# A retention block and two gated MLPs on one core: first loads held to three under way, first weights loaded and converted early, transposes of 64 rows in pairs, both banks of a phase as one tile

## The chip, the core and the metric

One core of a Trainium2 chip runs the whole program. Time is device microseconds (us) of one execution. The kernel before took a median of 939.42 us in 3 runs (938.97 to 939.46). The engines are PE (TensorE, with its weight loads as PEld), DVE (VectorE), ACT (ScalarE), POOL (GpSimd) and SP (SyncE, which here only issues DMAs). [...]

## The reference

Float32 throughout. Retention over 4 sequences of 576 positions with 8 heads of 64, then two MLPs over all 2304 tokens:

```python
gamma = 1.0 - 2.0 ** (-5.0 - np.arange(H))
Dmat = np.where(rel >= 0, gamma[:, None, None] ** rel, 0.0)      # rel = i - j
attn = ((q @ k.T) / sqrt(64) * Dmat) @ v                         # per sequence and head
x = attn as [2304, 512]
h = x @ w_in;  x = (h * sigmoid(1.702 * h)) @ w_out              # 512 -> 2048 -> 512
xn = x / sqrt(mean(x * x) + 1e-6) * rms_g
out = (silu(xn @ w_gate) * (xn @ w_val)) @ w_out2                # 512 -> 1536 -> 512
```

## The kernel before

**Tiling.** The tokens are cut into 18 units of 128 (two chunks of 64; `units`, L216). The MLPs work on blocks of 512 or 384 tokens (`BLOCKS`, L19). Matrix products of the MLPs are three passes over float32 values split into a high and a low part (`three`, L206). Weights arrive as 512 KB loads in six staging slots (`w_load`, L138), and `conv` (L168) turns each into such parts: two ACT instructions in place (L171, L172), one DVE instruction (`ww`, L181), then the high part (L188) and the low part (L191). With `rest` given, L188 runs on ACT and L191 is kept for a later call.

**A unit of attention** has three phases. `a_trans` (L259) transposes k and q on PE against an identity, ACT copies kT out of PSUM (L271), DVE multiplies qT by decay (L272) and POOL multiplies v by decay in place (L273). `a_scores` (L285) makes the 64x64 score blocks (L292) and the products of k and v (L301); DVE masks the scores into r (L307). `a_state` (L314) carries the running state S on DVE. `a_out` (L343) multiplies r by v (L352) and S by qT (L364); ACT copies x out of PSUM (L373), DVE adds the other half (L377), ACT and POOL or DVE split x into xh (L381) and xl (L383).

**Order.** Each engine runs its instructions in the order in which the code records them (`manual_schedule`). The front (L678 to L707) handles units 0 to 3 alone, phase after phase; then block 0 of the first MLP runs with its weight conversions and the phases of units 4 to 7 between its steps (L732), and blocks 1 to 3 run with the phases of units 8 to 17.

**Loads.** SP issues all loads in program order. The loads of units 0 to 3 stand there one after the other; those behind them go through `held` (L670): after each load, `behind` (L664) has SP issue a DMA of one word out of the load three before (`scrap`, L667), so that SP waits until that load has landed. Such a DMA reads the tile, so an instruction that later writes the tile in place (L273 for v, L171 and L172 for a staging slot) also waits until it is done.

**PSUM in the front.** A phase takes two tiles of one bank each (`a_psum`, L255): transposes from the pool `ps_at`, scores and outputs from `ps_acc`.

## Time and profile before

| | |
|---|---|
| median of 3 runs | 939.42 us (938.97 to 939.46) |
| profiled execution, and its span | 937.07 us, 935.3 us |
| PE busy | 922.1 us (99%) |
| DVE, ACT, POOL busy | 536.3, 377.6, 44.2 us (57%, 40%, 5%) |
| chain that ended last | PE 90%, DVE 5%, ACT 3%, issue 2% |
| transposes on that chain (L264) | 1% |

The span falls into three stretches: the front up to the first MLP matmul at 28.74 us, block 0 with the weight conversions up to about 130 us, and the rest. A time in the timeline is the start from the span's beginning and then the duration; what stands in brackets is the engine's idle time before it and what ended it ("issue" is a wait for nothing that the profile shows). Matmul durations overlap, so the pace of PE is read from start to start.

### The profile page before, as it was taken

What the parts mean: (1) busy time and instruction counts of PE and PEld (TensorE: products, weight loads), DVE (VectorE), ACT (ScalarE), POOL (GpSimd) and SP (SyncE); (2) the same over time, 40 slices, a digit from 0 to 9 for tenths busy, and PEclk for the clock granted to TensorE, in tenths of its full rate; (3) what the DMA queues carried; (4) which work ended last, traced back from release to release, by engine and by line L of the source; (5) the groups of instructions that cost most, each with busy time, mean ns of one, the idle gap of its engine ahead of it and who ended that gap; (6) DMA issues with size and microseconds to landing.
All of it is one profiled execution on the core that took longest, in us unless ns stands there. A gap on an engine that the chain in (4) does not pass through costs nothing.

```text
span 935.3 us, 15298 instructions
## 1 busy us (share of the span) xinstructions
PE 922.1 (99%) x6356; PEld 799.4 (85%) x6356; DVE 536.3 (57%) x885; ACT 377.6 (40%) x682; POOL 44.2 (5%) x47
## 2 busy tenths in 40 slices
PE   8899999999999999999999999999999999999998
PEld 7677788888999999988888888888888889999997
DVE  4888774444568555567777647464444544644333
ACT  3666654333444444466565523322332223223222
POOL 3111110000010010000000000000000000000000
PEclk9899999999999999999999999999999999999999
DMA  9866612101411324054455300200020001000000
GB/s 218 262 192 188 169 35 69 35 12 23 125 35 35 93 56 147 2 169 121 136 172 192 100 1 1 80 1 0 1 79 1 1 0 46 1 1 1 35 1 34
DMA packets 91579, 67.06 MB, mean 72 GB/s; under 512 B 58868, under 2 KB 81652, under 8 KB 91510
## 3 DMA queue, kind: packets, MB, share of 16 engines
q1 hardware_dynamic: 91074, 65.94, 23.8%
q8 instruction: 50, 0.82, 0.4%
q10 hardware_dynamic: 436, 0.14, 0.1%
q14 instruction: 19, 0.16, 0.1%
HBM read 55.59 MB, written 10.49 MB: 71 GB/s over the span
## 4 chain that ended last, share of the span: by engine, by line
PE 90%; DVE 5%; ACT 3%; issue 2%; DMA 0%; ACTq 0%; DVEq 0%
PE h L209 12%; PE acc L210 11%; PE acc L211 11%; PE acc L209 11%; PE h L211 11%; PE h L210 11%; PE v L209 5%; PE v L210 5%; PE v L211 5%; PE at L264 1%; DVE ww L181 1%; PE at L364 1%; PE at L292 1%; PE at L352 1%; DVE w L181 1%
## 5 line engine op out<-in xcount | busy, mean ns | idle before, releaser
L209 PE MATMUL h<-xh,w 128*128 128x512 f32 (+1 forms) x560 | 212.4, 379 | 2.1 <-ACT xh L381 2.1
L210 PE MATMUL h<-xl,w 128*128 128x512 f32 (+1 forms) x560 | 206.9, 369 | 0.3 <-DVE xl L383 0.3
L211 PE MATMUL h<-xh,w 128*128 128x512 f32 (+1 forms) x560 | 206.8, 369 | 0.0
L395 ACT CAST gh<-g 128x512 fp32r<-128x512 f32 (+1 forms) x140 | 80.9, 578 | 235.8 <-DVE g L546 152.9
L397 DVE TENSOR_TENSOR gl<-g,gh 128x512 fp32r<-128x512 f32 (+1 forms) x140 | 92.0, 658 | 79.5 <-ACT gh L395 79.5
L209 PEld LDWEIGHTS h<-xh,w 128*128 128x128 f32 x560 | 105.6, 188 | 18.6 <-ACT xh L381 2.4
L210 PEld LDWEIGHTS h<-xl,w 128*128 128x128 f32 x560 | 105.6, 189 | 14.9 <-issue 1.3
L203 DVE TENSOR_TENSOR wrl<-w,wrh 128x512 fp32r<-128x512 f32 x130 | 92.1, 709 | 45.5 <-ACT wrh L202 44.6
L211 PE MATMUL acc<-gh,wrl 128*128 128x512 f32 (+1 forms) x320 | 117.6, 367 | 0.0
L210 PE MATMUL acc<-gl,wrh 128*128 128x512 f32 (+1 forms) x320 | 117.5, 367 | 0.0
L209 PE MATMUL acc<-gh,wrh 128*128 128x512 f32 (+1 forms) x320 | 117.5, 367 | 0.0
L211 PEld LDWEIGHTS h<-xh,w 128*128 128x128 f32 x560 | 105.5, 188 | 13.5
L202 ACT CAST wrh<-w 128x512 fp32r<-128x512 f32 x130 | 80.4, 618 | 60.5 <-PE acc L211 45.1
L419 DVE TENSOR_TENSOR g<-h,g 128x512 f32<-128x512 f32 (+1 forms) x80 | 50.9, 636 | 72.8 <-ACT g L418 72.7
L209 PE MATMUL v<-xh,w 128*128 128x512 f32 (+1 forms) x240 | 88.1, 367 | 0.0
L210 PE MATMUL v<-xl,w 128*128 128x512 f32 (+1 forms) x240 | 88.1, 367 | 0.0
L211 PE MATMUL v<-xh,w 128*128 128x512 f32 (+1 forms) x240 | 88.1, 367 | 0.0
L418 ACT ACTIVATE g<-h 128x512 f32<-128x512 f32 (+1 forms) x80 | 44.2, 553 | 102.1 <-PE h L211 102.0
L211 PE MATMUL acc<-wrh,gl 128*128 128x512 f32 x216 | 84.5, 391 | 0.0
L210 PE MATMUL acc<-wrl,gh 128*128 128x512 f32 x216 | 84.5, 391 | 0.0
L209 PE MATMUL acc<-wrh,gh 128*128 128x512 f32 x216 | 84.0, 389 | 0.0
L543 DVE TENSOR_TENSOR g<-h,g 128x512 f32<-128x512 f32 (+1 forms) x60 | 38.2, 637 | 68.7 <-ACT g L542 68.6
(88 smaller groups left out, 1126.6 us busy)
## 6 DMA issues: line engine op xcount, KB each, us to landing
sslots<-in_moe_w_out_dram SPq DMA_DIRECT2D x28, 512.0 KB, 3.9
sslots<-in_moe_w_in_dram SPq DMA_DIRECT2D x16, 512.0 KB, 3.9
sslots<-in_moe_w_gate_dram SPq DMA_DIRECT2D x12, 512.0 KB, 3.9
sslots<-in_moe_w_val_dram SPq DMA_DIRECT2D x12, 512.0 KB, 4.3
out_dram<-sslots SPq DMA_DIRECT2D x17, 256.0 KB, 2.2
k<-in_k_dram SPq DMA_DIRECT2D x16, 256.0 KB, 3.4
q<-in_q_dram SPq DMA_DIRECT2D x16, 256.0 KB
v<-in_v_dram SPq DMA_DIRECT2D x16, 256.0 KB, 5.6
```

The lines of the kernel that those rows point to most:

```text
L181: nc.vector.scalar_tensor_tensor(out=w.bitcast(U32), in0=hi.bitcast(U32), scalar=3, in1=lo, op0=ALU.logical_shift_left, op1=ALU.bitwise_or,)
L202: nc.scalar.copy(out=wh.bitcast(F32R), in_=w)
L203: nc.vector.tensor_tensor(out=wl.bitcast(F32R), in0=w, in1=wh, op=ALU.subtract)
L209: nc.tensor.matmul(ps, lh, rh, start=first, stop=False)
L210: nc.tensor.matmul(ps, lh, rl, start=False, stop=False)
L211: nc.tensor.matmul(ps, ll, rh, start=False, stop=last)
L264: nc.tensor.transpose(pt[i][:, p * 128:(p + 1) * 128], t[:, 2 * p:2 * p + 2, :].rearrange("p h d -> p (h d)"), ident,)
L395: nc.scalar.copy(out=gh, in_=g)
L397: nc.vector.tensor_tensor(out=gl, in0=g, in1=gh.bitcast(F32), op=ALU.subtract)
L418: nc.scalar.activation(out=g, in_=ps, func=AF.Sigmoid, scale=1.702)
L419: nc.vector.tensor_tensor(out=g, in0=ps, in1=g, op=ALU.mult)
L543: nc.vector.tensor_tensor(out=g, in0=pg, in1=g, op=ALU.mult)
```

## The change

The loads of all four first units go through `held`, and the first 512 KB of `w_in` go right behind unit 0's k, q and v. Its conversion is recorded after unit 0's scores, its low part after unit 1's transposes. A transpose of 128 rows becomes two of 64 rows (chunk c reads its 64 partitions and writes bank c). The two banks of a phase are one tile of the program, so that kT, r and x leave PSUM in one instruction each, and the front draws all its phases from one pool of three such tiles; the pools for the accumulators and for the later phases are opened after the front.

```diff
     def a_psum(where):
         pool, tag = where
-        return [pool.tile([128, 512], F32, tag=tag, name="at") for _ in range(2)]
+        return pool.tile([128, 2, 512], F32, tag=tag, name="at")
     def a_trans(u, where):
-        for i, t in ((1, kr), (0, qr)):
+        for i, t in enumerate((kr, qr)):
             for p in range(HP):
-                nc.tensor.transpose(pt[i][:, p * 128:(p + 1) * 128], t[:, 2 * p:2 * p + 2, :]..., ident)
+                for c in range(2):
+                    cs, at = slice(C * c, C * c + C), (i * HP + p) * C
+                    nc.tensor.transpose(pt[:, c, at:at + C], t[cs, 2 * p:2 * p + 2, :]..., ident[cs, cs])
-        nc.scalar.copy(out=kT, in_=pt[1])
-        nc.vector.tensor_tensor(out=qT, in0=pt[0], in1=qdec, op=ALU.mult)
+        nc.scalar.copy(out=kT, in_=pt[:, :, :HP * C])
+        nc.vector.tensor_tensor(out=qT, in0=pt[:, :, HP * C:], in1=qdec..., op=ALU.mult)
...
-        for j in range(2):
-            nc.vector.tensor_tensor(out=r[j], in0=sc[j][:, :HP * C]..., in1=mask..., op=ALU.mult)
+        nc.vector.tensor_tensor(out=r, in0=sc[:, :, :HP * C]..., in1=for_mask, op=ALU.mult)
...
-        for c in range(2):
-            nc.scalar.copy(out=xc[c], in_=po[c][:, :HP * C])
+        nc.scalar.copy(out=x..., in_=po[:, :, :HP * C])
...
-        a_load(0, "kq")
-        a_load(0, "v")
...
-        a_load(3)
+        held(0, "k", "q", "v")
         held(None)
+        held(1, "k", "q", "v")
+        held(2, "k", "q", "v")
+        held(3, "k", "q", "v")
         held(4, "k", "q")
...
-        a_scores(0, ACC)
+        a_scores(0, FRONT)
+        conv_next(1, N2, rest=rest)
         a_state(0, (0,))
         for u in range(1, 4):
-            a_trans(u, AT)
+            a_trans(u, FRONT)
+            if u == 1:
+                rest.pop()()
...
-        conv_next(1, N2, rest=rest)
-        a_state(3, (1,))
-        a_out(3, ACC, rest.pop())
+        a_out(3, FRONT)
+        ps_front.__exit__(None, None, None)
+        ps_acc = ctx.enter_context(tc.tile_pool(name="ps_acc", bufs=4, space=PSUM))
+        ps_at = tc.tile_pool(name="ps_at", bufs=1, space=PSUM)
         a_trans(4, AT)
```

What SP issues first, before (k, q, v of units 0 to 3, 256 KB each, then a weight load of 512 KB):

```order
L247 DMA k<-in_k_dram 128x8x64
L247 DMA q<-in_q_dram 128x8x64
L247 DMA v<-in_v_dram 128x8x64
L146 DMA sslots<-in_moe_w_in_dram 128x4x256
L250 DMA k<-in_k_dram 64x8x64 x2
L250 DMA q<-in_q_dram 64x8x64 x2
L146 DMA sslots<-in_moe_w_in_dram 128x4x256
L667 DMA scrap<-sslots 1x1
```

(The first three rows stand there four times before the weight load.) Now:

```order
L246 DMA k<-in_k_dram 128x8x64
L246 DMA q<-in_q_dram 128x8x64
L246 DMA v<-in_v_dram 128x8x64
L145 DMA sslots<-in_moe_w_in_dram 128x4x256
L668 DMA scrap<-k 1x1
L246 DMA k<-in_k_dram 128x8x64
L668 DMA scrap<-q 1x1
L246 DMA q<-in_q_dram 128x8x64
L668 DMA scrap<-v 1x1
L246 DMA v<-in_v_dram 128x8x64
L668 DMA scrap<-sslots 1x1
```

The weight load moved ahead of nine loads, and a one-word read stands before each load of units 1 to 3.

POOL in the front, with the semaphores that an instruction waits for (DMAHW ones are DMAs), before:

```order
L273 TENSOR_TENSOR v<-v,vdec 128x512 [waits DMAHW5_49,DMAHW2_49,Pool_49]
L273 TENSOR_TENSOR v<-v,vdec 128x512 [waits DMAHW0_49]
L383 TENSOR_TENSOR xl<-x,xh 128x4x128 [waits Activation_49]
L273 TENSOR_TENSOR v<-v,vdec 128x512 [waits DMAHW3_49]
L383 TENSOR_TENSOR xl<-x,xh 128x4x128 [waits Activation_49]
L273 TENSOR_TENSOR v<-v,vdec 128x512 [waits DMAHW6_49]
```

Now:

```order
L277 TENSOR_TENSOR v<-v,vdec 128x512 [waits DMAHW3_49,DMAHW5_49,DMAHW2_49,Pool_49]
L277 TENSOR_TENSOR v<-v,vdec 128x512 [waits DMAHW4_49,DMAHW3_49]
L383 TENSOR_TENSOR xl<-x,xh 128x4x128 [waits Activation_49]
L277 TENSOR_TENSOR v<-v,vdec 128x512 [waits DMAHW2_49,DMAHW1_49]
L383 TENSOR_TENSOR xl<-x,xh 128x4x128 [waits Activation_49]
L277 TENSOR_TENSOR v<-v,vdec 128x512 [waits DMAHW1_49,DMAHW0_49]
```

Each product of v waits for one DMA more: the one-word read of that v.

DVE from unit 0's qT to unit 1's r, before and now:

```order
L272 TENSOR_TENSOR qT<-at,qdec 128x512 [waits PE_49,Activation_49]
L307 TENSOR_TENSOR r_235<-at,mask 128x4x64 [waits PE_49,Pool_49]
L307 TENSOR_TENSOR r_236<-at,mask 128x4x64 [waits PE_49]
L331 COPY S<-at 128x256
L272 TENSOR_TENSOR qT<-at,qdec 128x512 [waits PE_49]
L339 TENSOR_TENSOR S<-at,S 128x256 [waits DVE_49]
L340 TENSOR_TENSOR S<-S,sdec 128x256 [waits DMAHW3_49,DVE_49]
L377 TENSOR_TENSOR x<-at,x 64x256 [waits DMAHW0_49,Activation_49]
```

```order
L274 TENSOR_TENSOR qT<-at,qdec 128x512 [waits Activation_49]
L309 TENSOR_TENSOR r<-at,mask 128x512 [waits PE_49,Pool_49]
L180 SCALAR_TENSOR_TENSOR ww<-sslots 128x512 [waits DMAHW6_49,Activation_49]
L332 COPY S<-at 128x256
L274 TENSOR_TENSOR qT<-at,qdec 128x512 [waits Activation_49]
L190 TENSOR_TENSOR w<-ww,w 128x512 [waits DVE_49]
L340 TENSOR_TENSOR S<-at,S 128x256 [waits DVE_49]
L341 TENSOR_TENSOR S<-S,sdec 128x256 [waits DMAHW3_49,DVE_49]
L377 TENSOR_TENSOR x<-at,x 64x256 [waits DMAHW0_49,Activation_49]
```

The conversion (ww and its low part w) stands between r and unit 1's qT, and qT waits for ACT (the copy of kT out of the same tile) where it waited for PE.

## Rows read from the trace of the kernel before

**Rows 1.** Busy time by stretch: start:end length, then engines, clock, DMA share, GB/s

```profile
28.74:130.00 101.26, 97.59 (x859) 79.59 (x860) 82.92 (x134) 64.91 (x121) 12.18 (x9) 0.93 0.61 179
130.00:383.00 253.00, 253.00 (x2385) 228.97 (x2384) 136.69 (x238) 102.06 (x191) 21.06 (x19) 0.95 0.21 59
```

**Rows 2.** Chain that ended last, in order of time, at block 0's beginning

```profile
30.34 0.70 DVE ww L181
```

**Rows 3.** What PE waited for from 28.74 to 400 us: total, times, longest

```profile
PE at L292 <- DVE qT L272: 2.9, 3, 1.1
```

**Rows 4.** Timeline of POOL: start, duration, instruction, in brackets the idle time before

```profile
5.88 1.04 POOL L273 TENSOR_TENSOR v<-v,vdec 128x512 f32<-128x512 f32 x1 [3.00 <-DMA v<-in_v_dram]
...
31.20 1.19 POOL L273 TENSOR_TENSOR v<-v,vdec 128x512 f32<-128x512 f32 x1 [5.93 <-DMA scrap<-v]
```

**Rows 5.** Timeline of SP at the end of the front

```profile
28.30 0.42 SPq L667 DMA_DIRECT2D scrap<-v  x1
```

**Rows 6.** The page's DMA issues: KB each, median us to landing

```profile
v<-in_v_dram SPq DMA_DIRECT2D x16, 256.0 KB, 5.6
```

**Rows 7.** Timeline of DVE in the front

```profile
10.20 0.76 DVE L307 TENSOR_TENSOR r<-at,mask 128x256 f32<-128x256 f32 x2 [1.46 <-PE at L301]
...
11.21 0.68 DVE L272 TENSOR_TENSOR qT<-at,qdec 128x512 f32<-128x512 f32 x1
11.80 0.41 DVE L339 TENSOR_TENSOR S<-at,S 128x256 f32<-128x256 f32 x1
...
13.55 0.76 DVE L307 TENSOR_TENSOR r<-at,mask 128x256 f32<-128x256 f32 x2 [0.22 <-PE at L301]
...
23.14 0.75 DVE L307 TENSOR_TENSOR r<-at,mask 128x256 f32<-128x256 f32 x2
...
25.09 0.73 DVE L181 SCALAR_TENSOR_TENSOR ww<-sslots 128x512 uint32<-128x512 uint32 x1 [0.87 <-ACT sslots L172]
...
27.91 0.67 DVE L191 TENSOR_TENSOR w<-ww,w 128x512 fp32r<-128x512 f32 x1
```

**Rows 8.** Timeline of ACT at the end of the front

```profile
25.85 0.62 ACT L188 CAST w<-ww 128x512 fp32r<-128x512 f32 x1 [0.79 <-DVE ww L181]
26.38 0.64 ACT L373 COPY x<-at 128x256 f32<-128x256 f32 x2
...
28.59 0.58 ACT L271 COPY kT<-at 128x512 f32<-128x512 f32 x1
```

**Rows 9.** Timeline of PE in the front

```profile
18.70 0.21 PE L301 MATMUL at<-v,k 64*64 64x64 f32 x1 [1.61 <-issue]
...
24.42 1.15 PE L364 MATMUL at<-qT,S 64*64 64x64 f32 x31
...
28.74 0.50 PE L209 MATMUL h<-xh,w 128*128 128x512 f32 x1 [2.14 <-ACT xh L381]
```

**Rows 10.** Timeline of PE before unit 12's transposes, then a weight load behind them

```profile
256.07 0.34 PE L211 MATMUL acc<-gh,wrl 128*128 128x384 f32 x1
...
257.14 0.19 PEld L210 LDWEIGHTS h<-xl,w 128*128 128x128 f32 x1
```

**Rows 11.** Timeline of PE around unit 11's scores, then of its weight loads

```profile
240.45 0.39 PE L211 MATMUL acc<-gh,wrl 128*128 128x512 f32 x1
240.77 0.69 PE L292 MATMUL at<-qT,kT 64*64 64x64 f32 x32
241.29 0.65 PE L301 MATMUL at<-v,k 64*64 64x64 f32 x32
...
241.86 0.19 PEld L209 LDWEIGHTS h<-xh,w 128*128 128x128 f32 x1
241.97 0.19 PEld L210 LDWEIGHTS h<-xl,w 128*128 128x128 f32 x1
```

**Rows 12.** Timeline of the weight loads of unit 1's first three transposes

```profile
10.01 0.14 PEld L264 LDWEIGHTS at<-ident,k 128*128 128x128 f32 x1
10.07 0.25 PEld L264 LDWEIGHTS at<-ident,k 128*128 128x128 f32 x2
```

## The prediction

> **What bounds the kernel now.** I read the page's busy times and slices first: PE is busy 99% of the span, so a change counts only where PE waits, or where PE's own work gets shorter. The 40 slices show PE below full in the first slice only. Then I took the busy times of two stretches [rows 1]. From 130 to 383 us PE is busy for all 253.00 of 253.00 us; the changed transposes of units 8 to 17 lie there, ten of the eighteen, and they pay in full. From 28.74 to 130 us PE lacks 3.7 us (101.26 less 97.59), and the chain that ended last runs through DVE and ACT from 30.34 us on [rows 2]: weights are converted there as fast as these two manage, and PE's waits for qT before a unit's scores come to 2.9 us [rows 3]. So block 0 ends earlier only if that loop starts earlier or turns faster. The front, before the first MLP matmul at 28.74 us [rows 9], is a chain from unit to unit through r. Behind 383 us nothing is changed.

> The sum is made against the profiled execution, 937.07 us; the median of the runs is 2.35 us above it, and I add that at the end.

> **Held loads: the first unit pays.** POOL's product of v(0) starts at 5.88 us, when v(0) lands [rows 4]. Now it also waits for the one-word read of v(0). SP cannot begin that read before v(0) has landed, and the issue of q(1) stands just ahead of it, so I take 6.3 us. How long such a read takes is seen once beside its waiter: SP began one at 28.30 [rows 5] and POOL started on it at 31.20 [rows 4], 2.9 us later. The other end is the 5.6 us from issue to landing of a v load in the queues [rows 6]. I take 3.3, near the first, with a little for the 512 KB weight load that now stands in the queues: v(0) free at 9.6 us (9.2 to 11.9). Behind it come POOL's product, 1.04 us [rows 4], and the kv products on PE, 0.57 from 241.29 to 241.86 [rows 11], with some 0.2 of hand-overs: r(0) at 11.4 us where it was 10.20 [rows 7], +1.2. Behind the waiting v(0), POOL holds only v(1) and xl(0), which nobody needs so soon. The reads of v(1) to v(3) cost me nothing: each is issued some 4 us apart, and POOL has done them before PE's scores of that unit end. That cover is gone if they take the 5.6.

> **First conversion in the front.** Between r(0) and r(1) DVE and ACT now carry: r 0.68 (by qT, which has its size), ww 0.73 [rows 7], the cast 0.62, kT 0.58 [rows 8], qT 0.68, which must wait for kT, then on DVE the low part 0.67 and three instructions of about 0.41 (two on S, one on x) [rows 7]. That is 5.2 us; starts overlap ends by some 0.05 each, so 5.0. It was 3.35 (10.20 to 13.55) [rows 7]. So r(1) is at 16.4 instead of 13.55. From r(1) to r(3) took 9.59 us (13.55 to 23.14) [rows 7], of which PE's wait of 1.61 before 18.70, for nothing that the profile shows [rows 9], is not the change's doing and I leave it out: 3.99 a unit. One instruction for two saves 0.06 each at r and at the copy of x (0.75 for two, 0.68 for one of that size), so 3.9: r(3) at 24.2 against 23.14, +1.06.

> **End of the front.** There the conversion is gone: the copy of x started at 26.38, 0.8 us behind the end of PE's products at 25.57 (24.42 and 1.15) [rows 9], because the cast stood ahead of it from 25.85 [rows 8]; and the low part at 27.91 leaves DVE [rows 7]. This gives back about 0.8. But kT(4) now comes later: its transposes take the tile that unit 3's sums are read from, wait for them, and qT(4) waits for kT. Adding up, the first conversion of block 0, at 30.34 before [rows 2], starts near 30.85: +0.5, and the loop of block 0 shifts by it. In block 0, r and x as single instructions save about 0.2 in all on the loop; PE's transposes there hide in its waits. I keep +0.3 for front and block 0. Its ends: all of the +1.06 passes on, or the 0.8 and the hole of 1.61 both come off (-1.4).

> **Transposes of 64 rows in blocks 1 to 3.** Ten times, on PE's path. Before: from the matmul ahead of a unit's transposes to the weight load of the second matmul behind them, 1.07 us (256.07 to 257.14) with 384 columns ahead [rows 10], so 1.13 with 512. The nearest rows for 64-row work are unit 11's scores [rows 11]: 0.32 from the last 512-column matmul to the first 64-row one; 0.57 for the 32 matmuls from 241.29 to the weight load at 241.86, which is 8 groups of four at some 0.058 (64 columns each, a little over half of the 0.11 that 128 columns take in [rows 12]) and about 0.10 until the array is free; 0.11 for that load. Sixteen half transposes stream 64 columns each; two of one pair use different row halves, so 8 pairs like those 8 groups: 0.57. With 0.06 for the first weight load (10.01 to 10.07) [rows 12]: 0.32 + 0.06 + 0.57 + 0.11 = 1.06 against 1.13, -0.07, times ten -0.7 us. Bounds: no overlap in the pairs, 8 times 0.058 more, +0.4 each or +4.0 in all; no drain on either side, -0.37 each or -3.7. I take the value by the scores, the nearest rows.

> These rows show a price for changing the mode: 0.32 into the 64-row work, 0.57 for 8 groups of 0.058. [...]

> **Sum.** 937.07 + 0.3 - 0.7 = 936.7, and with 2.35 about 939.0 for the median. What can be told from no change here is 0.2%, or 1.9 us: 937.5 to 941.3.

> **Rivals.**
> First, slower: the reads land late. If the one-word reads take the 5.6 us, v(0) is free at 11.9 and r(0) starts 2.3 us later than in my sum; the conversion's weights wait behind it on DVE, and everything to block 0 shifts: 939.0 + 2.3 to 2.5 = 941.4. It decides from a landing of about 11.8 on. For it: loads with the reads' queues full take that long [rows 6]. Against: the one read that was waited for took 2.9 [rows 4, 5]. Chance 0.22.

> Second, slower: pairs that don't overlap. The weight loads of the 128-row transposes follow each other 0.11 apart once they stream (0.25 for two of 0.14 each) [rows 12]. If a half transpose pays for its 128 weight columns as a whole one does, a pair takes 0.11 at best where I took 0.058: 8 times 0.05, +0.4 a unit, +4 in all, 943.0. Against: the first load in the same rows is followed after 0.06, and the scores' 32 loads of 64 columns fit into 0.57 [rows 11]. Chance 0.08. [...]

> Third, faster: the front gains. With three loads under way, fewer bytes stand before each read; if v(0)'s word is back 1.2 us earlier than I took, r(0) stays at 10.20. PE's scores then also come 0.3 us sooner in two or three cycles because r and x leave in one instruction while the low part falls into PE's time: -1.2 and -0.6, 937.2. For it: the cycle before holds only 3 us of DVE work. Against: five instructions more stand between r(0) and r(1). Chance 0.26.

> **How the numbers follow.** Forecast 0.44 (its own range 937.6 to 940.9), late reads 0.22, pairs 0.08, front gains 0.26. Faster by over 0.2%: the third rival, 0.26. Within: 0.44. Slower: 0.22 + 0.08 = 0.30. The range goes from 936.0, a little below the third rival, to 943.0, the second; above it are only both slower cases together.

> **What would show it.** In the timeline of the changed kernel: POOL's v(0) ends its wait on the read of scrap at 9 to 10 us; r starts at about 11.4, 16.4, 20.3 and 24.2; DVE's qT waits for ACT's kT; the first conversion of block 0 at about 30.85; PE's waits for qT in block 0 no longer than 2.9 us together; from the matmul ahead of a unit's transposes in blocks 1 to 3 to the load of the second behind 1.0 to 1.1 us. I am wrong if POOL waits beyond 11.8, if a unit's sixteen transposes start over more than 0.6 us, or if the stretch from 130 to 383 us changes by over 2 us with no change at the transposes.

## The result and the profile after

The changed kernel took a median of 942.49 us (942.38 to 944.81, 5 runs), the kernel before 938.97 (934.88 to 939.46) beside it: a ratio of 1.0056, 95% interval 1.0037 to 1.0075. So it is slower, where no change was forecast (939.0). The profiled execution took 944.81 us, the slowest of these runs; before it was 937.07. The difference between the two profiles is therefore 7.7 us, where the medians differ by 3.5 and the ratio says about 5.

The first MLP matmul starts at 37.14 us instead of 28.74 [rows 9], 8.4 us later. From there on nothing is lost: counted from that matmul to the end of the execution, 907.7 us pass now and 908.3 passed before. The loss is all in the front. Of the 8.4 us, 3.2 lie before r(1) (16.73 where it was 13.55 [rows 7]), which the forecast had (2.85); 4.5 lie between r(1) and r(3), and 0.7 behind r(3).

PE in the changed kernel's timeline (start, duration, instruction, in brackets the idle time before and what ended it):

```profile
21.16 0.57 PE L303 MATMUL at<-v,k 64*64 64x64 f32 x21 [0.86 <-issue]
...
24.04 0.63 PE L294 MATMUL at<-qT,kT 64*64 64x64 f32 x24
29.45 0.38 PE L294 MATMUL at<-qT,kT 64*64 64x64 f32 x3 [4.79 <-issue]
...
36.09 0.69 PE L268 MATMUL at<-ident,k 64*128 64x64 f32 x8 [1.67 <-ACT x L373]
36.55 0.66 PE L268 MATMUL at<-ident,q 64*128 64x64 f32 x8
37.14 0.79 PE L208 MATMUL h<-xh,w 128*128 128x512 f32 x1
```

In the middle of unit 3's scores, with 24 of 32 matmuls done, PE stops for 4.79 us and waits for nothing that the profile shows. It is the same kind of stop as the 1.61 us of [rows 9], three times as long. The chain that ended last runs through it, and through the one before:

```profile
20.31 0.86 issue
...
24.66 4.79 issue
```

DVE's r and POOL's v in the same kernel:

```profile
9.46 1.04 POOL L277 TENSOR_TENSOR v<-v,vdec 128x512 f32<-128x512 f32 x1 [6.57 <-DMA q<-in_q_dram]
14.10 1.04 POOL L277 TENSOR_TENSOR v<-v,vdec 128x512 f32<-128x512 f32 x1 [3.60 <-DMA scrap<-v]
```

```profile
11.83 0.69 DVE L309 TENSOR_TENSOR r<-at,mask 128x512 f32<-128x512 f32 x1 [3.39 <-PE at L303]
...
16.73 0.67 DVE L309 TENSOR_TENSOR r<-at,mask 128x512 f32<-128x512 f32 x1
...
21.78 0.69 DVE L309 TENSOR_TENSOR r<-at,mask 128x512 f32<-128x512 f32 x1 [0.80 <-PE at L303]
...
30.84 0.69 DVE L309 TENSOR_TENSOR r<-at,mask 128x512 f32<-128x512 f32 x1 [5.02 <-PE at L303]
```

r(0) and r(1) stand within half a us of the forecast's 11.4 and 16.4; r(3) stands 6.6 us behind its 24.2. The windows (columns as in [rows 1]) of the changed kernel, then two of the kernel before:

```profile
20.00:30.00 10.00, 4.11 (x159) 3.66 (x161) 4.25 (x10) 2.41 (x4) 3.58 (x3) 0.96 0.89 238
30.00:40.00 10.00, 7.54 (x117) 6.49 (x110) 5.06 (x10) 3.96 (x7) 1.04 (x1) 0.52 0.65 201
130.00:383.00 253.00, 253.00 (x2404) 225.19 (x2403) 138.91 (x230) 103.75 (x184) 23.94 (x20) 1.00 0.22 61
```

```profile
20.00:30.00 10.00, 6.60 (x202) 5.72 (x203) 7.52 (x16) 5.66 (x13) 2.14 (x2) 0.93 0.98 260
30.00:40.00 10.00, 10.00 (x81) 7.93 (x81) 8.34 (x14) 7.03 (x13) 1.19 (x1) 0.82 0.94 326
```

Behind the stop PE's granted clock is 0.52 from 30 to 40 us (0.50 in the window from 29.30 to 39.50), where it was 0.82 before.

**What the stop is.** The windows give the number of PE's instructions up to the stop (matmuls in the first bracket, weight loads in the second). The kernel before has a second, short stop:

```profile
22.72 0.44 PE L301 MATMUL at<-v,k 64*64 64x64 f32 x11 [0.40 <-issue]
```

Up to its stops at 18.70 and 22.72 us:

```profile
0.00:18.00 18.00, 15.84 (x345) 13.13 (x346) 7.80 (x18) 5.86 (x12) 6.33 (x16) 0.97 0.92 212
0.00:22.60 22.60, 19.46 (x471) 16.30 (x471) 10.39 (x24) 7.60 (x15) 8.61 (x18) 0.97 0.91 214
```

And now, up to the stops at 21.16 and 29.45:

```profile
0.00:20.80 20.80, 16.95 (x349) 13.75 (x350) 8.64 (x17) 7.39 (x12) 6.32 (x16) 1.00 0.87 203
0.00:28.00 28.00, 20.20 (x476) 16.69 (x477) 12.13 (x24) 9.80 (x16) 9.90 (x19) 1.00 0.90 222
```

With the sequencer's own instructions, which no view counts (14 and 19 before, 6 and 8 now, by the trace), that is 705 and 961 in both kernels: 256 apart, at other places of the program. The page has a DMA queue named instruction; over the whole execution, before and now:

```profile
q8 instruction: 50, 0.82, 0.4%
```

```profile
q8 instruction: 51, 0.84, 0.4%
```

By the trace every packet of this queue has 16384 bytes, and PE has 12806 and 13045 instructions. If the queue brings PE's instructions alone, that is about 256 for each packet, an estimate from these counts (12806 / 50 = 256.1, 13045 / 51 = 255.8). Between the first stop's end and the second, in two windows of the changed kernel's DMA view:

```profile
q1 hardware_dynamic: 1577, 1.63, 97.4%
```

```profile
q1 hardware_dynamic: 1216, 0.30, 111.3%
q8 instruction: 1, 0.02, 5.7%
```

From 21.20 to 26.80 us no such packet, from 26.80 to 28.10 one (it starts at 26.84 and takes 1.19), and PE goes on 1.4 us behind its end. Before, PE passed instruction 705 at 18.70, the packet started at 20.04 and took 1.23, and PE could go on at 22.72, again 1.4 us behind its end. What SP had issued when PE passed 705 this time:

```profile
19.64 0.56 SPq L145 DMA_DIRECT2D sslots<-in_moe_w_in_dram  x1
...
20.64 0.40 SPq L145 DMA_DIRECT2D sslots<-in_moe_w_in_dram  x1
...
21.47 0.36 SPq L143 DMA_DIRECT2D sslots<-in_moe_w_out_dram  x1
```

**Theory A**: in the front PE lives on packets of 256 instructions, of which the next is asked for when PE begins the last one that it has; the change makes PE pass 705 (at 21.16) within a burst of three 512 KB loads, two of them issued and the third 0.3 us later, and the packet waits in turn behind them. No view shows when a packet is asked for; that is an assumption of the theory. **Theory B**: the longer chain, the held loads or the transposes make PE wait, whatever an instruction's number.

### The profile page after: what moved, and what is told of

Same layout as the page of the kernel before. It is cut to its first block, busy times and chain, and to the rows that moved or that the text cites. A ratio compares the mean times of both kernels' runs of the same rounds, so it can differ in the third digit from the quotient of the medians.

```text
span 942.7 us, 15504 instructions
## 1 busy us (share of the span) xinstructions
PE 923.0 (98%) x6500; PEld 796.7 (85%) x6500; DVE 534.4 (57%) x867; ACT 377.2 (40%) x664; POOL 44.4 (5%) x47
## 4 chain that ended last, share of the span: by engine, by line
PE 88%; DVE 5%; issue 2%; ACT 2%; DMA 1%; POOL 0%; SPq 0%; ACTq 0%; POOLq 0%
PE h L208 12%; PE acc L210 11%; PE acc L209 11%; PE acc L208 11%; PE h L210 11%; PE h L209 11%; PE v L210 5%; PE v L209 5%; PE v L208 5%; PE at L365 1%; DVE ww L180 1%; PE at L353 1%; DMA q<-in_q_dram 1%; DVE w L180 1%; PE at L294 1%
```

## The experiments

Ratios are to runs of the kernel before on the same chip, with the 95% interval. Except where told, an experiment starts from the changed kernel.

**The program moved by 116 instructions.**

```diff
-        warm_up(2)
+        for _ in range(31):
+            nc.tensor.matmul(heat[:32, :16], ones[:, :32], ones[:, :16], start=True, stop=True)
```

> The changed kernel with 31 tiny float32 matmuls (32x16) in place of the two warm-up matmuls between unit 0's transposes and scores, where PE waits for qT and v anyway: PE's program becomes 116 instructions longer there, nothing else changes. Theory A (PE runs out of instructions: it stops at its 705th and 961st instruction in both kernels, 256 apart, each time until a 16 KB instruction packet has come, and the packet asked for at 21.2 us stood behind three 512 KB loads): the stops move to other instructions, the 4.8 us before unit 3's scores go, a shorter one of at most 3 us may come at unit 3's products; r(3) starts at 25 to 27 us instead of 30.8, the first MLP matmul at 29 to 32 instead of 37.1, time 4 to 7 us under the changed kernel. Theory B (the longer chain with the conversion and the held loads keep PE waiting, whatever the instruction's number): stop and r(3) stay within 1 us, time within 1 us of the changed kernel.

940.55 us, ratio 1.0010 (0.9994 to 1.0025): no longer clearly slower than the kernel before, though PE has more to do; the median is 1.9 us under the changed kernel's, where 4 to 7 were expected. No stop at 705 or 961; one at 28.71 us, and the count up to it, 1209 and 8 of the sequencer, is 1217, again 256 on:

```profile
0.00:28.00 28.00, 22.71 (x604) 19.47 (x605) 13.80 (x28) 9.67 (x16) 10.17 (x19) 0.98 0.88 217
```

```profile
28.71 1.54 PE L365 MATMUL at<-qT,S 64*64 64x64 f32 x25 [0.88 <-issue]
```

r(3) is at 26.04 as A has it; h, the first MLP matmul, at 33.40, later than its 32. r(3) alone would not tell the theories apart (a run below has it at 26.64 with PE's program unchanged up to there); the place of the stop does, and theory B falls by it.

**Two loads, and five loads under way from unit 4 on.**

```diff
-            if len(marks) > 2:
-                i = len(marks) - 3
+            lag = 3 if len(marks) < 15 else 2        # 5 in the other run
+            if len(marks) >= lag:
+                i = len(marks) - lag
```

> The changed kernel, but from unit 4's first loads on two loads are under way and not three. Theory A: fewer bytes stand ahead of the instruction packet that is asked for at about 21 us, so it comes 1 to 2.5 us earlier (starts at 24.3 to 25.8 instead of 26.8), the stop before unit 3's scores falls from 4.8 to 2.3 to 3.8, time 1 to 3 us under the changed kernel. Theory B: the stop stays, time within 1 us or slower because loads come later.

> The changed kernel, but from unit 4's first loads on five loads are under way and not three; the opposite of the run with two. Theory A (PE's stops are waits for instruction packets that come in turn behind the loads): the packets asked for at instructions 705 and 961 start later than 5 us after the request, the stops at these instructions sum to 5 to 8 us, h at 37 to 40 us in the profile, time 0 to 3 us over the changed kernel. Theory B (bytes ahead don't matter): stops at 961 as in the run with two loads, 1.6 us, time as there.

Two: 942.51 us, 1.0027 (1.0009 to 1.0046), runs from 937.9 to 943.8; in the profiled one (939.68) the stop at 961 is 1.6 us and the packet starts at 23.00. Five: 942.72, 1.0050 (1.0032 to 1.0067), but the packet starts at 21.29, earlier and not later, 1.1 us behind PE's passing of 705 (20.18), and the stop is 1.0; there PE waits for POOL instead, since the read of v(3) now stands five loads behind it:

```profile
PE at L303 <- POOL v L277: 5.7, 3, 2.8
```

As a dose of loads these two fail: SP issues the first two of the three weight loads within a us of each other at 19.8 to 21.2 us in either. The packet's early start with five loads speaks against a wait set by the hold alone.

**The parts alone.** Transposes and joint tiles without the loads and the early conversion (which stands behind unit 3's scores again; the diff shows the loads only), and the reverse (loads, conversion and joint tiles with transposes of 128 rows):

```diff
-        held(0, "k", "q", "v")
-        held(None)
-        held(1, "k", "q", "v")
...
+        a_load(0, "kq")
...
+        a_load(3)
+        held(None)
```

```diff
-                for c in range(2):
...
+                nc.tensor.transpose(pt[:, i, p * 128:(p + 1) * 128], t[:, 2 * p:2 * p + 2, :]..., ident)
```

> Only the 64-row transposes and the joint tiles of the change; loads and the first conversion stand as in the kernel before. PE's instructions have the numbers of the changed kernel. Theory A: the request at instruction 705 comes at 17 to 19 us, before the 512 KB loads are issued, so no stop over 2 us; first MLP matmul at 28.3 to 29.8, time 936.5 to 939.5 (the kernel before less 0.5 for blocks 1 to 3). Theory B': the transposes or the joint tiles cost the time: 941 to 943.

> Only the held loads, the early first conversion and the joint tiles of the change; transposes have 128 rows, so PE's instructions have the numbers of the kernel before. Theory A: instruction 705 falls at the end of unit 2's kv products, at 20 to 22 us, the packet it asks for stands behind the 512 KB loads, and PE stops for 3 to 5 us at instruction 961, at the end of unit 3's kv products; time 941 to 944 and, without the gain of blocks 1 to 3, the stretch from 130 to 383 us 0.5 us longer than in the changed kernel. Theory B' (transposes or their count are the cause): no such stop, 937 to 939.

Transposes and tiles: 939.92 us, 1.0007 (0.9992 to 1.0023). Loads and conversion: 942.39, 1.0040 (1.0024 to 1.0057), with stops of 0.7 us at 705 and 2.5 at 961. So the larger part of the loss comes with the loads and the conversion. One expectation was wrong: the first has stops too, of 0.6 us at 449, 2.4 at 705 and 1.1 at 961, at the very counts of the changed kernel.

**The word read is one of q.**

```diff
-                behind(raws[what, nm][:1, 0, :1])
+                behind(raws[what, "q" if nm == "v" else nm][:1, 0, :1])
```

> The changed kernel, but behind a load of v SP reads one word of the unit's q and not of v, so POOL's product of v no longer waits for that read. Theory C (the read of v(0) is what made r(0) late): POOL starts v(0) at 5.5 to 7 us instead of 9.46, r(0) at 10.0 to 10.5 instead of 11.83, and r(1) 1.3 to 1.8 us earlier; the stop at instruction 961 stays in its place, so the time falls by 0 to 2 us only. Rival D (PE's scores are late for another reason): r(0) stays after 11.3.

941.92 us, 1.0037 (1.0023 to 1.0052). POOL starts v(0) at 5.88, and r(0) is at 10.62, 1.2 us earlier:

```profile
5.88 1.04 POOL L277 TENSOR_TENSOR v<-v,vdec 128x512 f32<-128x512 f32 x1 [2.99 <-DMA v<-in_v_dram]
```

So in the changed kernel it is the read of v(0) that holds POOL until 9.46, though the profile names a load of q there. r(2) is at 21.02, only 0.8 us earlier, since the stop at 705 is longer here (1.4 us; 3.4 at 961). The median is 0.6 us under the changed kernel's, which the intervals don't tell from nothing.

**Unit 4's transposes don't wait**, first by giving the warm-up a tile of the front's pool, then by taking unit 4's tile from that pool:

```diff
         a_out(3, FRONT)
+        a_trans(4, FRONT)
         ps_front.__exit__(None, None, None)
...
-        a_trans(4, AT)
```

> The changed kernel, but the warm-up's tile takes the first of the front's three tiles, so that unit 4's transposes write banks that unit 3's sums are not read from. Theory E (their wait for ACT's and DVE's sums, 1.7 us, puts them between unit 3's xh and the first MLP matmul): the transposes start right behind unit 3's products, the first MLP matmul comes 0.5 to 1.2 us earlier after r(3) (5.1 to 5.8 us where 6.3 passed), time 0 to 1.5 us under the changed kernel. Rival: h waits for xh anyway, and nothing changes.

> The changed kernel, but unit 4's transposes take their tile from the front's pool before it is closed, so that they no longer wait for unit 3's sums (the run with the warm-up's tile left that wait as it was). Theory E: the 1.7 us wait of PE before unit 4's transposes goes, they run right behind unit 3's products, r(3) to the first MLP matmul takes 5.0 to 5.8 us where 6.3 passed; stops at 705 and 961 as in the changed kernel; time 0 to 1.5 us under it. Rival: h waits for xh at the same time anyway, r(3) to h stays above 6.0.

The first left the wait of 1.7 us as it was: 943.03, 1.0041 (1.0023 to 1.0059), and says nothing on theory E. The second took it away: 942.33, 1.0039 (1.0019 to 1.0058). Of its 12 runs 4 lie under 940 and 8 over 941.9; the profiled one is of the low ones (939.37) and has a stop of only 0.49 us before the same instruction 961:

```profile
24.98 0.34 PE L294 MATMUL at<-qT,kT 64*64 64x64 f32 x6 [0.49 <-issue]
...
31.34 0.49 PE L208 MATMUL h<-xh,w 128*128 128x512 f32 x1 [1.68 <-ACT xh L381]
```

PE's program and the loads up to there are those of the changed kernel, so a stop's length differs from run to run. From r(3) to h 4.70 us pass (26.64 to 31.34), but the run with transposes and tiles alone, where unit 4's transposes do wait, has 4.70 too. Its two rows, behind r(3) of this run:

```profile
26.64 0.69 DVE L309 TENSOR_TENSOR r<-at,mask 128x512 f32<-128x512 f32 x1 [0.99 <-PE at L303]
```

```profile
25.78 0.69 DVE L309 TENSOR_TENSOR r<-at,mask 128x512 f32<-128x512 f32 x1 [1.18 <-PE at L303]
```

```profile
30.48 0.50 PE L208 MATMUL h<-xh,w 128*128 128x512 f32 x1
```

The granted clock from r(3) to h is 1.00 in both: at that clock h waits for xh anyway. In the changed kernel, and in five more runs with 6.30 to 6.31, it is 0.50.

**The first conversion late**, behind unit 3's scores:

```diff
-        conv_next(1, N2, rest=rest)
         a_state(0, (0,))
...
+        conv_next(1, N2, rest=rest)
+        a_state(3, (1,))
+        a_out(3, FRONT, rest.pop())
```

> The changed kernel, but the first conversion stands where it stood before, after unit 3's scores; loads are held and the first weight load is early as in the change. r(0) to r(1) falls from 4.9 to 3.2 to 3.8 us, since ACT's cast and DVE's ww and low part no longer stand between. By theory A this only moves the request at 705 by about a us: if it then comes before the 512 KB loads are issued the stop at 961 shrinks below 3 us and the time falls by 2 to 5 us; a fall of 1.5 us or less and the stop within 1 us of 4.8 would say that the conversion's place costs the time by its own length alone.

943.13, 1.0055 (1.0038 to 1.0073): nothing gained. r(0) to r(1) stays at 4.87 us, and the stop at 961 is 5.1. The expectation that the first would shorten was wrong: POOL can't start v(1) before the held read of it is back, and ends it at 15.50 us, where PE then waits:

```profile
14.46 1.04 POOL L277 TENSOR_TENSOR v<-v,vdec 128x512 f32<-128x512 f32 x1 [3.90 <-DMA scrap<-v]
```

```profile
15.55 0.69 PE L303 MATMUL at<-v,k 64*64 64x64 f32 x32 [0.52 <-POOL v L277]
```

The held read of v(1) stands behind the conversion as a second bound. This run says one thing more. It has the loads of the change without its early conversion, and its ratio is that of the changed kernel (1.0055 for 1.0056); the transposes and tiles with neither had 1.0007. So the loss comes with the held and reordered loads, and the early conversion adds none that can be seen.

**The 512 KB loads spread**, the burst taken apart:

```diff
         held(4, "k", "q")
         held(None)
-        held(None)
-        held(None)
         held(4, "v")
-        held(5, "k", "q", "v")
+        held(5, "k")
+        held(None)
+        held(5, "q", "v")
+        held(None)
```

> The changed kernel, but of the three 512 KB loads behind k and q of unit 4 only one stays there; the second comes behind v of unit 4 and k of unit 5, the third behind q and v of unit 5. Theory A (the instruction packet asked for when PE begins instruction 705 queues behind loads issued in a burst at 19.6 to 21.9 us): the packet starts at most 3.5 us after the request (5.7 in the changed kernel), the stop at instruction 961 falls from 4.8 to below 2.5 us, r(3) at 25.5 to 28, time 1 to 4 us under the changed kernel. Rival F (the packet is late for another reason than these loads): stop still 4 us or more.

939.29 us, 1.0013 (0.9997 to 1.0029), 3.2 us under the changed kernel's median by an order of loads alone; the interval doesn't meet the changed kernel's (1.0037 to 1.0075). In the profiled execution, 941.73, its slowest, the packet starts 3.7 us behind PE's passing of 705 (at 24.26) and the stop is 2.6, both just outside what was expected:

```profile
26.68 0.38 PE L294 MATMUL at<-qT,kT 64*64 64x64 f32 x3 [2.59 <-issue]
```

With the word of q and unit 4's transposes besides:

> The changed kernel with all three: a word of q instead of v is read behind v loads, the 512 KB loads spread, unit 4's transposes not waiting. By theories A, C and E the losses add up: r(0) at 10 to 10.6 us, stop at 961 below 2.5, r(3) at 24 to 27, h at 29 to 32, and the time 4 to 7 us under the changed kernel, 936 to 939, the kernel before within 0.2%. If the stops only move on to the next block of 256 instructions, 940 to 942.

939.47, 1.0020 (1.0002 to 1.0037), no better than the spread alone, where 936 to 939 were expected: r(0) at 9.09, but stops of 0.5 us at 705 and 2.9 at 961. The gains don't add up.

**More instructions in the kernel before.**

```diff
             a_scores(u, ACC)
+            for _ in range(10):
+                nc.tensor.matmul(heat[:32, :16], ones[:, :32], ones[:, :16], start=True, stop=True)
```

> The kernel before with 10 tiny float32 matmuls (32x16, 40 instructions on PE) behind the scores of units 1 to 3 each, where PE waits for r anyway; nothing else changes. Theory A (in the front PE lives on packets of 256 instructions, so instructions cost their share of a packet even where PE would wait): PE stops at its instructions 705 and 1217, the sum of its stops for nothing shown rises from 2.0 by 2 to 4 us, h at 31 to 33 instead of 28.74, time 2 to 5 us over the kernel before. Theory B (only PE's busy time and the waits between engines count): h within 0.6 us, no difference that can be measured.

940.27 us, 1.0030 (1.0013 to 1.0046), 1.6 us over the median beside it (938.65), a little less than the least expected. The stops are at the two instructions named (691 and 14 make 705, 1197 and 20 make 1217) and come to 3.4 us, where the kernel before has 2.0:

```profile
0.00:18.50 18.50, 16.86 (x345) 14.12 (x346) 6.50 (x16) 5.74 (x11) 6.34 (x16) 1.00 0.92 210
0.00:28.50 28.50, 24.04 (x598) 20.71 (x599) 12.94 (x31) 9.98 (x19) 9.89 (x19) 1.00 0.89 219
```

```profile
29.21 0.45 PE L364 MATMUL at<-qT,S 64*64 64x64 f32 x8 [2.09 <-issue]
```

**Fewer instructions, no holding, spread loads.** The run with all three and 128-row transposes in units 0 to 4; the same with the loads of units 0 to 3 and the conversion as before; and the kernel before with nothing but the spread loads (the diff above):

```diff
+        if u < 5:
+            ... nc.tensor.transpose(pt[:, i, p * 128:(p + 1) * 128], t[:, 2 * p:2 * p + 2, :]..., ident)
```

> The changed kernel with the word of q, the spread 512 KB loads and unit 4's transposes that don't wait, and with transposes of 128 rows in units 0 to 4: PE has 80 instructions fewer up to the first MLP matmul. Theory A: fewer instructions need fewer packets; the stops before the first MLP matmul sum to under 2.5 us (3.4 with 64-row transposes), h 0.5 to 2 us earlier, time 0.5 to 2 us under that run (939.5), 937.5 to 939. Rival: the count does not matter, 939 to 940.

> Loads of units 0 to 3 not held and the first conversion behind unit 3's scores, as in the kernel before; joint tiles, 64-row transposes from unit 5 on, unit 4's transposes not waiting, 512 KB loads spread. If held loads and early conversion are the other part of the loss, this is the kernel before or 0.3 to 1 us better: h at 28 to 29.5 us, 937.5 to 939. If the joint tiles themselves cost in the front, 940 or more.

> The kernel before with the three 512 KB loads spread as in the run with spread loads, nothing else. Theory A: there the packet that came 3.7 us after its request (at 22.72 us) was not needed before 36 us, so the time stays within 1 us of the kernel before. If it falls by over 1.5 us, the loads in a burst cost the kernel before as well.

They took 939.25 (1.0003, 0.9990 to 1.0015), 938.16 (0.9987, 0.9973 to 1.0000) and 936.99 us (0.9977, 0.9965 to 0.9989). The 80 instructions fewer come with stops of 1.5 us in the profile instead of 3.3, but the medians differ by 0.2 only: not shown by time. The last is 2.3 us faster than the kernel before, which theory A as I had it did not expect. Its profile (938.33, over its median) still shows a stop of 2.12 us at instruction 705; why the median falls is not shown by it:

```profile
19.55 0.21 PE L301 MATMUL at<-v,k 64*64 64x64 f32 x1 [2.12 <-issue]
```

**What is settled.** In all 17 profiles the time behind the first MLP matmul is 906.7 to 908.3 us, so the front makes nearly all of the difference. That PE's stops are waits for instruction packets is shown: these profiles have 29 stops of PE over 0.2 us for "issue" before the first MLP matmul, all at instruction 449, 705, 961 or 1217 (to within two), whatever matmul that is, and each ends 0.96 to 1.60 us behind the end of a 16 KB packet. That the order of the loads costs time is shown by the spread loads, at equal instructions, in both kernels.

That a burst costs it through longer stops is likely and not shown: the stop at 961 came to 0.5, 1.0, 1.6, 3.2, 3.4, 4.8 and 5.1 us in seven profiles with 64-row transposes, held loads and the burst, and to 2.6 and 2.9 with the loads spread. Nor is it settled what sets a packet's wait. It started from at once to 6.2 us behind PE's passing of 449, 705 or 961, and once 9.4 behind 1217. The order of the queue, as theory A has it, fits most runs and fails in one pair. With five loads under way and with the late conversion, PE passes 705 just before SP issues the first of the three loads (20.18 and 20.35, 19.88 and 19.97), and the packet starts 1.1 us later in the one run and 6.2 in the other.

## Why the prediction was wrong, step by step

**The step that failed** stands under "First conversion in the front": "PE's wait of 1.61 before 18.70, for nothing that the profile shows [rows 9], is not the change's doing and I leave it out: 3.99 a unit." So the sum has the stop at nothing: it gives r(1) to r(3) 7.8 us where 9.59 had passed, and 1.61 of that gain is something for which the change gives no reason. Kept as it was, the stop would have put r(3) at 25.8 and the sum 1.6 us higher. The runs show that it is a wait for instructions, and that the loads which the change reorders bear on the time: 0.86 and 4.79 us now, 5.65 where the sum has none. With it fell r(2) (21.78 for 20.3) and r(3) (30.84 for 24.2). The view showed the stop and gave no cause; I took a wait without a cause for one that would go. The lower end of that step (-1.4) even takes the 1.61 off a second time, since the +1.06 lacks it already.

**A price that is in no term of the sum** is the granted clock: r(3) to h takes 6.30 us at 0.50, and 4.70 at 1.00 in the two runs compared above, 1.6 us more. It fell to 0.50 at 29.30 us, at the end of the 4.79 us in which PE did nothing and the clock was 1.00. That the long stop brought it down is not shown: with the program moved by 116 instructions it was 0.50 from 27 us on, ahead of that run's only stop, and with five loads under way it was 0.50 from r(3) to h behind a stop of 1.0 us.

Against the profile the two make up most of the miss: 936.7 of the sum, 5.65 and 1.6 are 944.0, and 944.81 was measured. That execution is the slowest of its five; the median is 3.5 us over the forecast's 939.0, and how long the stops of the faster runs were no profile tells.

**Held loads, the first unit**: right. v(0) free at 9.46 (9.6 forecast), r(0) at 11.83 (11.4); a word of q instead gives 1.2 us back at r(0). That the reads of v(1) to v(3) cost nothing was right here (0.2 us of PE's waits), but only because the conversion covers v(1); without it r(1) comes no sooner behind r(0).

**First conversion**: 5.0 us from r(0) to r(1) forecast, 4.90 measured.

**End of the front**: the first conversion of block 0 starts at 39.01 instead of 30.85, most of it by the stops and the clock of 0.50. PE's wait of 1.7 us for unit 4's tile was foreseen, and at a clock of 1.00 it cost nothing (4.70 us from r(3) to h with it and without it).

**Transposes in blocks 1 to 3**: right in sign and near in size. With 384 columns ahead, PE in the changed kernel and then its second weight load behind:

```profile
263.24 0.33 PE L209 MATMUL acc<-gl,wrh 128*128 128x384 f32 x1
263.42 0.34 PE L210 MATMUL acc<-gh,wrl 128*128 128x384 f32 x1
263.68 0.46 PE L268 MATMUL at<-ident,k 64*128 64x64 f32 x8
263.98 0.42 PE L268 MATMUL at<-ident,q 64*128 64x64 f32 x8
```

```profile
264.44 0.19 PEld L209 LDWEIGHTS h<-xl,w 128*128 128x128 f32 x1
```

1.02 us (1.07 in [rows 10]), and 1.07 with 512 columns (1.06 forecast, 1.13 before). Ten units give -0.5, where -0.7 was forecast, and -0.3 against the run with loads and conversion and 128-row transposes, whose granted clock is 1.00 as here and not the 0.95 of [rows 1]. The pairs overlap (sixteen starts within 0.49 us, the two of a pair 0.003 to 0.005 apart), so the second rival is out. The price into the 64-row work is there, as forecast: 0.26 us from the last 384-column matmul to the first transpose, where those matmuls follow each other every 0.18. Into the 128-row transposes of the kernel before it was 0.18 (from 256.07 in [rows 10]):

```profile
256.25 0.61 PE L264 MATMUL at<-ident,k 128*128 128x128 f32 x4
```

What PE does in that time no view shows; that it drains was the author's assumption. The lower bound of that step (-3.7) seems to leave out the last load's 0.11 in each unit as well; with it, it is about -2.6.

**The rivals.** The first had the time nearly (941.4), by luck and not by its mechanism: the read of v(0) was back in time. The third did not come: v(0)'s word was back no earlier than in the sum. None of the three says what the stop would do. Of the signs named beforehand only the last two starts of r failed, and the conversion behind them; POOL's wait (9.46), the transposes (0.49 us) and PE's waits for qT in block 0 (2.9 us) came as forecast.

**A reading of the page** was wrong beside it: the 40 slices show PE under 90% in the first two and in the last, not in the first only. No term hangs on it.

## What to carry to other kernels

Where PE runs many small matmuls while loads are under way, count its instructions too, with their weight loads: a stop "for nothing that the profile shows" that lies at the same count at other places of the program, or 256 apart, and ends just behind an instruction packet (0.96 to 1.60 us here), was a wait for instructions in these kernels. Adding 116 instructions moved it from 705 and 961 to 1217. The place of the program is what to check: the changed kernel has one more such wait, 1.2 us at 51.91 in block 0, which lies behind 1393 instructions now and behind 1315 in the run with loads and conversion and 128-row transposes, both times before unit 4's products with r. So it hangs on the place and not on the count, and its cause is open. Don't leave such a wait out of a sum, and don't carry it over as a constant either: bound it, and look at the engine's granted clock behind it. Try spreading large loads between small ones before holding them back: that took the ratio to the kernel before from 1.0056 to 1.0013 for the changed kernel, and to 0.9977 for the kernel before itself.
